# One fewer turned head (21 for 22), a new written order for the attention loop, and rows of maxima split by ScalarE and GpSimd in place of VectorE

## The chip, the core and the metric

The kernel runs on one core of one Trainium2 chip, as one program. The metric is the device time of one execution in microseconds (us), the median of several runs. TensorE (PE in the profile) multiplies matrices into PSUM, PEld is its loading of weights, VectorE is DVE, ScalarE is ACT, GpSimd is POOL, and SP is the queue that issues most DMAs.

## What is computed

One token block of 2048 rows and 448 columns: a layer norm, 16-head attention with one shared key and value (head width 28), an MLP on a second layer norm, and a sum of all.

```python
xn = _layernorm(x)
q = (xn @ wq).reshape(B, S, 16, 28).transpose(0, 2, 1, 3)
k, v = xn @ wk, xn @ wv
p = softmax(einsum("bhqd,bkd->bhqk", q, k) * 28 ** -0.5)
A = einsum("bhqk,bkd->bhqd", p, v).transpose(0, 2, 1, 3).reshape(B, S, 448) @ wo
B = gelu(_layernorm(xn) @ w1 + b1) @ w2 + b2
return x + A + B
```

All of it is float32. The kernel splits operands into a rounded high part and a low part (names ending in h and l) and adds the products.

## The kernel before

The 2048 rows are four chunks of 512 queries, the 16 heads four groups of four: a **unit** is one chunk and one group, 16 units in all, and a head of a unit is written (u, j). A score matrix is needed twice: once for the maximum of each row of queries, once with its exponentials as weights of the values.

There are three stages. First come layer norms and projections, which leave q in DRAM (`qd`) and the keys and values in SBUF (`ks`, `vs`). Then the MLP runs, 56 slots of TensorE work, and into it are mixed steps of two streams that belong to attention:

- `m`, a step of `max_stream` (lines 659 to 675): one matmul `m<-ks,qm` of 128 queries by 512 keys (L669), whose row maxima VectorE takes from PSUM (L670). A head has 16 of them. When a unit is through, its maxima are gathered in `mr` (L674).
- `t`, a step of `turned_scores` (lines 696 to 718) for a **turned** head: the same matmul (L706), but VectorE writes the scores themselves to the buffer `raw`, permuted, with their row maximum (L707, and L713 after four steps). Four `t` steps fill one `raw`. Two steps `x` (`turned_exp`, lines 720 to 730) take exponentials in place on ScalarE (L724), and after the second SP stores `raw` in DRAM as `td` by four DMAs (L727). There are two such buffers in the attention stage, so the first `t` of a chunk writes where the chunk before the last one is being stored from.

The third stage is attention, over units in order, written out by hand in the table `ORDERS`: 64 strings, four for a unit, each for four blocks of 128 keys. Each letter is one step:

- `s`, `score` (lines 1113 to 1126): for a head that isn't turned, keys by queries, one matmul `m<-xh,ks` (L1124), exponentials from PSUM into `p` on ScalarE (L1125).
- `T`, `turn_blocks` (lines 1095 to 1103): for a turned head no matmul and no exponential is left. The stored block comes back into `quarter` by DMA (L928, on SP, after a small memset L927), and VectorE transposes it in 32 by 32 squares into two `p` tiles (L1100).
- a digit: so many blocks of keys times values, `po<-p,vs` (`pv`, lines 1078 to 1093; L1088, four heads side by side in the array, eight instructions for a block).
- `m`, `t`, `x` as above; `n`, a step of the normalisation of a finished unit; `o`, four columns of the output projection (L959 to L961); `e`, `load_max` of the next unit; `|`, the next pair of blocks begins and its DMAs are issued.

So a head that is turned costs TensorE 16 matmuls (`t`) and VectorE 16 evictions and 8 transposes; one that isn't costs TensorE 32 (`m` and `s`), VectorE 16 reductions and ScalarE 16 exponentials. `TURNED` lists the turned heads, 22 of 64: head 3 of each unit, and head 2 of units 4, 7, 9, 11, 13 and 15.

`load_max` (lines 645 to 657) puts the negative maxima of a unit as two more rows under its queries, a rounded part and the rest, so that the score matmul subtracts them. TensorE turns `mr` into a row (L649), ScalarE writes the rounded part from PSUM (L652), VectorE the rest (L655), and two DMAs copy them into `qs` (L656 and L657), on POOL's queue in this stage.

PSUM has seven banks for the small results (`m0` to `m6`, by the table `BANKS`, one digit for each result) and one for `po`. Each engine runs its instructions in the order written. What a matmul waits for is thus the bank's last reader, VectorE or ScalarE.

Of the kernel before, what the change touches and what calls it, by code (L numbers as in the profile page):

```python
# [10 lines left out]
F32 = mybir.dt.float32  # L11
F32R = mybir.dt.float32r
AF = mybir.ActivationFunctionType
ALU = mybir.AluOpType
# [3 lines left out]
P = 128  # L18
S, D, H, DH, F = 2048, 448, 16, 28, 1792
NT = S // P  # L20
CT = 4
# [5 lines left out]
SCALE = DH ** -0.5  # L27
PAIRS = 13
ORDERS = (
    "ssmsmsmssTsssmmss2s|T",  # L30
    "msmsststtstTssssTsssx|",
    "|ssxTt5esmstsstmsssmsTss",
    "tsssx|Tx4tsmsssmttsstTssxs",
    "sxssTsss5mnmstsntssn|nsmsmT",
    "T|sss3smsmstmssmmsTsss",
    "snssTsms4nTeststsssnmssn|",
    "mmxn|xTsnmtmnm4nTssntmsssmstsssss",
    "Tmxss12sTsmss|ssssss",
    "2|nTmxsttsnnnstTsm2stemssssmxsss",
    "mnTssmn4nnm|xsststssttnsTmssss",  # L40
    "sxms4T|xtsmnssmsmmsstssmssT",
    "mnnTst3s|ssmsnmmsstsmsxTsss",
    "t|m3nmtsmntxsmnTsss2ssTmsssmmss",
    "tsTsm2msnmsmessnnnsstsmt|Tm2mnsmss",
    "nmsnmnsmtmmmT4mxmxsmsmssmssnsns|smTs",
    "sTs6nnTTmsm|snmsosmsnnosT",
    "sTTsTssTm|5sesss",
    "nstnsnsTsTTss4Tnt|ss",
    "smsTnT|xsmosssTmxTns4nos",
    "stssmstssmtnmsoxmx|Tssts3tststT",  # L50
    "ssTsnosTsms|m4xnestssntomsstms",
    "ssmnnmtosTmmxsssnT24xnnxnmssmmsms|ss",
    "mmmsnsssmtnttsos|nmmsnmmsstmxsTssT",
    "Txs6Tmmsmmmtmnomstsmsmsssmmnstt|nsss",
    "s|stnTxtmm3smmssxnttsxmTmsnsns3mmsss",
    "s|msTsssTmmxotmssmssmmsss",
    "Tmnnmsmnm3smstmsnemmstm3Tmmssnmss|mssts",
    "Txmmostms|msmssTnsT4Tmss",
    "mntsnsmsTTssss6nnnsT|T",
    "T|mnmensstmnsnsssTsxnTsT",  # L60
    "ssss6sTTTntmsm|Tss",
    "ss|mn1ssmtsstTsmnxxsmsssm3Tmsmtm",
    "nssts|momnxmnsTmxsTn5mestsosntntsnssms",
    "tsssmsT2smsmnsmn|smmsnmsTss",
    "ssxsmxnTsmnm3smsmms|stmsTstss",
    "TTnmmss6Tts|mnmnnmssTmsss",
    "sTsm|4TnestsmsnTssTns",
    "ssTsTssnTTxo6smnmss|",
    "snmmssxTsTsTssosTmt4nnnn|",
    "sststssssmmTsmssm|2ttmstsxmT",  # L70
    "nsxssmomn3smnmsm|smsmstsmsTsTs",
    "ts|mtTs5omstnsomosnmxmsmmmnxomtsmstssmmsxTmms",
    "m4esmnssnmstnTmtxtomnTmsmnosmmssmmssmstm|ns",
    "TtTsotstTnmssmm4nsnms|msmTs",
    "T|sstnsxTxTxms5ensnTmsnss",
    "ssnTsnxTTss5Ts|msms",
    "smssmnsmsm|TmnmsnTTTss",
    "sss2snstttssTsnt4nmtomssso|sTx",
    "nTnx|s4ensomssmsmmnsmssmsmmTssnmomosn",
    "ss|3sTtssmsnsnmsmtTtstsossm",  # L80
    "Tms4snmssmnnstsnsmstts|sTmmssx",
    "sT|ss6onTTsmnxmTonossss",
    "sTsnmsTs4msTmoTs|nmsmmts",
    "ssTsTss|Tme6sTssnt",
    "ssmsxntmsmxommnTt|mnsonmTsTsTs",
    "ssmmsxxn4snntTsmssmsm2tn|msnssmmmTs",
    "sstsnntTsxnssT7nmxsmssmmsmss|mm",
    "nsssssmsnsmmn3esTs|Tsss",
    "|ssss1nsssTsTss5ss",
    "sTTnnssTsssssnT2nn|",  # L90
    "sTsTnssssTn31sTs|",
    "Tsss|sTsosTo7Tss",
    "TT|ssssoTsssTos",
)
BANKS = (
    "0163240516324501634205163420516324510632451603245160342561034256103425160423156042315604213650241365"
    "0241365240615324061352406153204651304265130246150324610532461053246105243061524301652345014623501462"
    "3054123065412306541236054123604512306542130654201635420163542013652401365240136542061345201643502614"
    "3502641532061453620145326014352601432560124356012345061243506124356012453610243561024356102345610234"
    "6510342653106534210654312065142305631420561304526130452613045261304251634025314602351460253146023154"  # L100
    "6203145620314560231456203164520316425063142560341256304125634021653402615304261530412654310265431026"
    "5304216503426150346231504625301642503614253061254306215340621530461320546123540612345062315034162503"
    "6421036452103642510364251034621530462153064215036145206134562301456320146523106241503640215630412536"
    "0412563420514635201463520146325041632540162350421560326041532061435206415302415630241563024153620416"
    "2054136203625410356421035642103546120531426314052361402536015365420136542013562410324561034256103642"
    "5103642510326541032654130256143206512430651243506124501362450163254013562401356241053621045236415023"
    "641502364150236415023415023415023415203415203"
)
# [11 lines left out]
def block_kernel(ctx, tc, x, wq, wk, wv, wo, w1, b1, w2, b2, out):  # L120
    nc = tc.nc
    pe, act, dve, pool = nc.tensor, nc.scalar, nc.vector, nc.gpsimd
    ctx.enter_context(tc.manual_schedule())

    def f(t):
        return t.bitcast(F32)
# [10 lines left out]
    def heads_of(u):  # L137
        return 4 - sum(v == u for v, _ in TURNED)

# [438 lines left out]
    for c in range(NCH):  # L578
        if c + 1 < NCH:
            center, turn = norm_parts(c + 1, False, bank=lambda shape: (qbank, mtile)[next(turns) % 2](shape))  # L580
        for i in range(4):
# [24 lines left out]
            if i in ((1, 3), (1, 2), (1, 3), (0, 2))[c]:  # L606
# [38 lines left out]
    def load_max(u):  # L645
        qs, mr = qss[u], mrs.pop(u)
        nh = heads_of(u)
        pm = mtile([nh * CT, P])
        pe.transpose(pm, mr[:, 0:nh * CT], ident)  # L649
        mn = keep.tile([4 * CT, 2, P], F32R, name="mn", bufs=1)[0:nh * CT]  # L650
        if u:
            act.activation(mn[:, 0, :], pm, AF.Copy, scale=-1.0)  # L652
        else:
            dve.tensor_scalar(mn[:, 0, :], pm, -1.0, 0.0, op0=ALU.mult, op1=ALU.add)
        dve.scalar_tensor_tensor(mn[:, 1, :], pm, -1.0, f(mn[:, 0, :]), op0=ALU.mult, op1=ALU.subtract)  # L655
        loads.dma_start(f(qs[60:61, 0:nh, :]), f(mn[:, 0, :]))  # L656
        loads.dma_start(f(qs[124:125, 0:nh, :]), f(mn[:, 1, :]))  # L657

# [38 lines left out]
    def turned_scores(i):  # L697
        for t in range(CT):
# [5 lines left out]
            for n in range(4):  # L704
# [4 lines left out]
                                  op0=ALU.mult, op1=ALU.max, accum_out=m3[:, n:n + 1])  # L709
                if (t, n) == (0, 3) and 0 < i < len(TURNED) - 1:  # L710
                    load_m(*TURNED[i + 1], q3[1 - i % 2])
                if n == 3:
                    dve.tensor_reduce(m3[:, 4:5], m3[:, 0:4], axis=AX.X, op=ALU.max, negate=True)  # L713
                    exps.extend((TURNED[i], t, raw, m3, h) for h in range(2))
                yield
# [127 lines left out]
    for n in range(len(mslots) + 2):  # L843
# [30 lines left out]
        ts, pace = 0, 21  # L874
# [28 lines left out]
    att = ctx.enter_context(tc.tile_pool(name="att", bufs=2))  # L903
# [253 lines left out]
    for n0 in range(0, len(steps), 2):  # L1157
        u, kt0 = steps[n0]
# [67 lines left out]
```

## Time and profile before

| | |
|---|---|
| median of 3 runs | 1044.84 us (1043.79 to 1046.39) |
| the profiled execution's own time | 1043.82 us |
| its span, first to last instruction | 1041.7 us |
| granted TensorE clock | 1.00 |
| first attention score (L1124) | 482.1 us into the span |
| DMA moved | 250.65 MB |

In the rows of a profile, a group has its line, engine, operation and names (out<-in), the number of instructions, the busy time in us, the mean duration of one in ns, and the idle time of the engine ahead of it with what ended it. A matmul's end is modelled, so TensorE's busy time and the mean of 400 ns for a 512-column matmul say little; the distance from one matmul's start to the next says what it costs. A row of the timeline has start and length in us, and consecutive instructions of one kind are merged, with their count.

### The profile page before, as it was taken

Reading aid. Unit: us, or ns where it says so; the run is one execution under the profiler, and the core shown is the slowest. Engines: PE = TensorE matmul, PEld = TensorE weight load, DVE = VectorE, ACT = ScalarE, POOL = GpSimd, SP = SyncE. Lnnn points to the kernel's source line nnn. Section 1 sums busy time; section 2 is a strip of 40 time slices with the busy share of each in tenths; the row PEclk is TensorE's granted clock in tenths of the full one; section 3 lists DMA queues with packets and bytes.
Section 4 is the critical chain, followed back from the end, with each engine's and each line's share of the span. In section 5 each row is a group of like instructions: output and inputs, shape, how many; then the busy total and the mean of one; then the engine's idle time right before and its main releaser. Section 6 shows DMA issues by size and latency. Waiting matters only on the chain.

```text
span 1041.7 us, 17889 instructions
## 1 busy us (share of the span) xinstructions
PE 1032.2 (99%) x5725; PEld 701.7 (67%) x5725; DVE 944.9 (91%) x1973; ACT 727.1 (70%) x1212; POOL 576.2 (55%) x716
## 2 busy tenths in 40 slices
PE   9999999999999999999999999999999999999998
PEld 8778888888888878887454544556454465556555
DVE  7889999999999999999797999899999999997975
ACT  6765555676767756565989878777687766776782
POOL 6679787767766777866163454244444435433420
PEclk9999999999999999999999999999999999999999
DMA  8866455888988887985989899979999999998991
GB/s 275 254 209 167 126 133 147 225 219 233 244 227 216 218 219 196 258 239 164 261 243 257 242 288 301 283 209 289 283 279 313 293 287 296 293 288 284 279 344 46
DMA packets 253202, 250.65 MB, mean 241 GB/s; under 512 B 19774, under 2 KB 216508, under 8 KB 253108
## 3 DMA queue, kind: packets, MB, share of 16 engines
q1 hardware_dynamic: 240884, 229.23, 75.2%
q0 software_dynamic: 10816, 19.70, 7.1%
q8 instruction: 45, 0.74, 0.3%
q10 hardware_dynamic: 1408, 0.57, 0.2%
q14 instruction: 49, 0.40, 0.1%
HBM read 141.14 MB, written 107.07 MB: 238 GB/s over the span
## 4 chain that ended last, share of the span: by engine, by line
PE 94%; DMA 2%; DVE 2%; issue 1%; POOL 1%; ACT 1%; SPq 0%; DVEq 0%; POOLq 0%
PE po L1088 19%; PE m L1124 15%; PE m L669 15%; PE m L789 13%; PE ph L263 11%; PE m L706 8%; PE qp L263 3%; PE m L959 1%; PE ph L266 1%; PE ph L268 1%; PE m L961 1%; PE m L960 1%; DMA td<-raw 1%; PE po L1071 1%; PE m L1071 1%
## 5 line engine op out<-in xcount | busy, mean ns | idle before, releaser
L670 DVE TENSOR_REDUCE mx<-m 128x1 f32<-128x512 f32 x672 | 430.2, 682 | 31.3 <-PE m L669 29.3
L1125 ACT ACTIVATE p<-m 128x512 f32<-128x512 f32 x578 | 300.7, 633 | 55.5 <-PE m L1124 54.5
L669 PE MATMUL m<-ks,qm 128*128 128x512 f32 x672 | 257.3, 400 | 1.7 <-DVE a L794 0.7
L1088 PE MATMUL po<-p,vs 128*32 128x512 f32 x1664 | 221.2, 595 | 0.0
L1124 PE MATMUL m<-xh,ks 128*128 128x512 f32 x672 | 217.0, 407 | 0.0
L707 DVE TENSOR_SCALAR_CACHE_REDUCE raw<-m 128x512 f32<-128x512 f32 x304 | 200.7, 685 | 18.0 <-PE m L706 7.9
L1100 DVE STREAM_TRANSPOSE p<-quarter 128x1024 f32<-128x1024 f32 x149 | 178.4, 1223 | 2.2 <-DMA quarter<-td 1.7
L724 ACT ACTIVATE raw<-raw,m 128x1024 f32<-128x1024 f32 x152 | 170.8, 1164 | 3.0 <-DVE m L713 1.9
L1124 PEld LDWEIGHTS m<-xh,ks 128*128 128x128 f32 x672 | 122.3, 188 | 65.3 <-ACT p L1125 15.2
L669 PEld LDWEIGHTS m<-ks,qm 128*128 128x128 f32 x672 | 124.9, 188 | 44.8 <-issue 9.2
L706 PE MATMUL m<-ks,q 128*128 128x512 f32 x352 | 137.6, 399 | 2.0 <-DVE raw L707 1.8
L754 ACT ACTIVATE hx<-ph,b1t 128x512 f32<-128x512 f32 x55 | 37.9, 689 | 131.0 <-PE ph L268 91.5
L1088 PEld LDWEIGHTS po<-p,vs 128*32 128x32 f32 x1664 | 56.9, 109 | 106.2 <-issue 101.3
L770 POOL TENSOR_TENSOR hl<-hx,hh 128x512 fp32r<-128x512 f32 x56 | 72.7, 1298 | 31.3 <-ACT hh L768 31.1
L706 PEld LDWEIGHTS m<-ks,q 128*128 128x128 f32 x352 | 65.7, 188 | 26.5 <-DVE raw L707 4.2
L789 PE MATMUL m<-w2h,hh 128*128 128x448 f32 x224 | 81.3, 366 | 0.0
L789 PE MATMUL m<-w2h,hl 128*128 128x448 f32 x224 | 81.3, 367 | 0.0
L789 PE MATMUL m<-w2l,hh 128*128 128x448 f32 x224 | 81.2, 366 | 0.0
L758 POOL TENSOR_TENSOR hz<-hz,hx 128x512 f32<-128x512 f32 x56 | 72.8, 1300 | 4.6
L763 POOL TENSOR_TENSOR hx<-hx,hz 128x512 f32<-128x512 f32 x56 | 72.7, 1297 | 4.7
L1088 PE MATMUL po<-xh,vs 128*32 128x512 f32 x256 | 66.8, 596 | 0.0
L1125 ACT ACTIVATE xh<-m 128x512 f32<-128x512 f32 x94 | 52.0, 634 | 21.0 <-PE m L1124 20.8
(202 smaller groups left out, 1591.0 us busy)
## 6 DMA issues: line engine op xcount, KB each, us to landing
quarter<-td SPq DMA_DIRECT2D x170, 512.0 KB
td<-raw SPq DMA_DIRECT2D x304, 256.0 KB
td<-xl SPq DMA_DIRECT2D x48, 256.0 KB
qd<-qe SPq DMA_DIRECT2D x24, 256.0 KB
xh<-qd POOLq DMA_DIRECT2D x36, 168.0 KB, 6.0
a<-in_A_x_dram SPq DMA_DIRECT2D x24, 224.0 KB
qm<-qd POOLq DMA_DIRECT2D x84, 56.0 KB, 5.2
qm<-qd SPq DMA_DIRECT2D x84, 56.0 KB
```

Of the source, the lines that this page charges most:

```text
L263: pe.matmul(ps, w, v, start=(n == 0), stop=False)
L669: pe.matmul(pm, qm[:, t * P:(t + 1) * P], ks[:, n * CW:(n + 1) * CW], start=True, stop=True)
L670: dve.tensor_reduce(mx[:, CT * j + t, n:n + 1], pm, axis=AX.X, op=ALU.max)
L706: pe.matmul(sc, q3[i % 2][:, t * P:(t + 1) * P], ks[:, n * CW:(n + 1) * CW], start=True, stop=True)
L707: dve.tensor_scalar(raw[:, n].rearrange("p r (b i) -> p b r i", i=32), sc.rearrange("p (b r i) -> p b r i", r=4, i=32), SCALE, -3e38, op0= ...
L724: act.activation(raw[:, rs], raw[:, rs], AF.Exp, bias=m3[:, 4:5], scale=1.0)
L758: pool.tensor_mul(hz, hz, hx)
L789: pe.matmul(m2[k], h[:, k * P:(k + 1) * P], w[:, ft, :], start=(ft == 0 and i == 0), stop=(ft == NF - 1 and i == 2))
L1088: pe.matmul(po[32 * j:32 * j + 32, :], vs[:, kt, :], ps.pop((u, kt, j)), start=(kt == 0), stop=(kt == NT - 1))
L1100: dve.transpose(p.rearrange("p k (g j) -> p g k j", j=32), part[:, :, 32 * k:32 * k + 64].rearrange("p g (k j) -> p g k j", j=32))
L1124: pe.matmul(s, ks[:, kt * P:(kt + 1) * P], qss[u][:, j, :], start=True, stop=True)
L1125: act.activation(p, s, AF.Exp, scale=SCALE)
```

## The change

Unit 9 has one turned head instead of two, and units 10 and 11 change places: 21 turned heads. The table of steps and the table of banks are new throughout. `load_max` of units 2 to 15 has ScalarE copy the whole negative maxima to SBUF, and GpSimd makes the rounded part and the rest; units 0 and 1 use VectorE for both.

```diff
-    "ssmsmsmssTsssmmss2s|T",
+    "ssmsmsmsmmsTTss|ssss",
...
-    "0163240516324501634205163420516324510632451603245160342561034256103425160423156042315604213650241365"
+    "0163240516324503126450312645031246503215460235146023541063254120635412065342106503421650341265340126"
...
-TURNED = tuple((u, j) for u in range(16) for j in ((3, 2) if u in (4, 7, 9, 11, 13, 15) else (3,)))
+TURNED = tuple((u, j) for u in range(16) for j in ((3, 2) if u in (4, 7, 10, 13, 15) else (3,)))
...
         mn = keep.tile([4 * CT, 2, P], F32R, name="mn", bufs=1)[0:nh * CT]
-        if u:
-            act.activation(mn[:, 0, :], pm, AF.Copy, scale=-1.0)
+        if u > 1:
+            whole = att.tile([4 * CT, P], F32, name="whole", bufs=1)[0:nh * CT]
+            act.activation(whole, pm, AF.Copy, scale=-1.0)
+            pool.tensor_scalar(mn[:, 0, :], whole, 1.0, 0.0, op0=ALU.mult, op1=ALU.add)
+            pool.tensor_sub(mn[:, 1, :], whole, f(mn[:, 0, :]))
         else:
             dve.tensor_scalar(mn[:, 0, :], pm, -1.0, 0.0, op0=ALU.mult, op1=ALU.add)
-        dve.scalar_tensor_tensor(mn[:, 1, :], pm, -1.0, f(mn[:, 0, :]), op0=ALU.mult, op1=ALU.subtract)
+            dve.scalar_tensor_tensor(mn[:, 1, :], pm, -1.0, f(mn[:, 0, :]), op0=ALU.mult, op1=ALU.subtract)
```

Lines behind `load_max` stand 3 later in the changed kernel (L1124 becomes L1127). Counted through the built programs, the changed one has 688 scores `s` for 672, 688 steps `m` for 672, 336 steps `t` for 352, 168 exponentials of `raw` for 176, 168 transposes for 176, 16 stores of `td` fewer (336 for 352) and 8 loads of `quarter` fewer (162 for 170). Up to the first score TensorE's instructions are of the same kinds in the same numbers in both, 354 steps `m` and 228 steps `t` among them. From there the products `po` stand in 67 unbroken runs between other matmuls in both, and the memory of blocks waiting for them, `p`, is as large as before.

The first place is `load_max` for unit 3 in GpSimd's queue (`oc` and `oth` belong to the normalisation of the unit before, `xh<-qd` and `qm` are loads of queries, `rc`, `ld` and `tr` carry the sums of the normalisation). Before:

```order
L634 DMA xh<-qd_99 28x3x512 x2
L569 DMA qm_166<-qd_98 28x512 x2
L569 DMA qm_166<-qd_99 28x512 x2
L992 DMA rc<-oc 128x1x16
L656 DMA xh<-mn 1x12x128
L657 DMA xh<-mn 1x12x128
L996 DMA ld<-rc 128x16
L1000 DMA tr<-ld 32x512 x4
```

After, at the same unit:

```order
L634 DMA xh<-qd_98 28x3x512 x2
L995 DMA rc<-oc 128x1x16
L999 DMA ld<-rc 128x16
L654 TENSOR_SCALAR mn<-whole 12x128
L655 TENSOR_TENSOR mn<-whole,mn 12x128
L659 DMA xh<-mn 1x12x128
L660 DMA xh<-mn 1x12x128
L1003 DMA tr<-ld 32x512 x4
L569 DMA qm_164<-qd_97 28x512 x2
```

Two small operations on 12 partitions now stand ahead of the two DMAs, and the loads of the sums and of the next queries stand behind them.

The second place is the reuse of a `raw` buffer, on VectorE. The changed order has at the start of unit 6 (`raw` is written by the turned step of line 710, `mx` are maxima, the number behind m_ names the PSUM result read):

```order
L673 TENSOR_REDUCE mx<-m_7869 128x1
L673 TENSOR_REDUCE mx<-m_7875 128x1
L673 TENSOR_REDUCE mx<-m_7878 128x1
L930 MEMSET quarter 1x1
L710 TENSOR_SCALAR raw,m_7821<-m_7894 128x4x4x32
L716 TENSOR_REDUCE m_7821<-m_7821 128x1
L673 TENSOR_REDUCE mx<-m_7902 128x1
L673 TENSOR_REDUCE mx<-m_7915 128x1
L710 TENSOR_SCALAR raw,m_7919<-m_7920 128x4x4x32
```

And ScalarE there, where the row of `raw` with m_7665 is the second exponential of the buffer that the last row above writes again:

```order
L727 ACTIVATE raw<-raw,m_7665 128x1024
L968 ACTIVATE ot<-m_7852 128x448
L1128 ACTIVATE p<-m_7872 128x512
L1128 ACTIVATE p<-m_7885 128x512
L1128 ACTIVATE p<-m_7888 128x512
L1128 ACTIVATE p<-m_7891 128x512
L1128 ACTIVATE p<-m_7905 128x512
L1128 ACTIVATE p<-m_7908 128x512
```

Between the exponential and the next writing of the same buffer VectorE has eight rows, from m_7869 on; TensorE has there the matmuls of these results, and right behind the four turned matmuls a run of 40 `po` instructions. The order before has, at the place of its chunk that waited for the store (unit 5, after `load_max`), this on VectorE, from the last row ahead of the chunk on:

```order
L670 TENSOR_REDUCE mx<-m_7598 128x1
L655 SCALAR_TENSOR_TENSOR mn<-m_7620,mn 12x128
L707 TENSOR_SCALAR raw,m_7631<-m_7632 128x4x4x32
L707 TENSOR_SCALAR raw,m_7631<-m_7641 128x4x4x32
L949 MEMSET a 1x1
L670 TENSOR_REDUCE mx<-m_7647 128x1
L707 TENSOR_SCALAR raw,m_7631<-m_7656 128x4x4x32
```

The run of `po` stands ahead of the chunk there, and behind it in the new order.

More of the change, by code (lines that the diff above doesn't have):

```diff
@@ L44 @@
[L44 to L93, printed above, removed]
+    "ssmsmsmsmmsTTss|ssss",
+    "ssTTs5tsstssmtsssmsst|",
+    "sTxTmstsx4esmsmsts|mstssss",
+    "sss|tTs3sTmssmtssstmsxs",
+    "sxsT|ssm4mmsstmsnssTtsss",
+    "nsns21T|esmntsmstnsssmTsssxs",
+    "|sTn4nsmsmsststmnxssxssss3nT1",
+    "ssTmm|msnmssmmsmTnsmssx2smmsnstmn",
@@ new lines @@
+    "sstssssmtT3mmmsmsss|nTtss",
+    "ssssT|n2nsmsmstnsssmsnsT",
+    "Tmnmsxsm|4xnensmnnnssmsttssmsssTs",
+    "sssnsT4Tsmsmsmssss|sn",
+    "mtmxTms|Ttxm6mmsmsmsnnnnssssssss",
+    "|T2Tmnmsssmsmmtssnnsnsssss",
+    "|Tte2sstsnsmsttssmmtxtmmmTx4smssmsmns",
+    "|sxmsssTmTms4msmmnsmsssss",
+    "ntTsTmtssn4Tmmnnmsssm|Tmss",
+    "ssTsTsnTnons4s|tsesT",
+    "Tsssnsms|TTmnn6sTss",
+    "sTs|ssTTxmsT4mmssmnms",
+    "s|smsmmTsnnss1snsmnmtssmTss",
+    "sssmo1tmxmm|nsTm3xsntsnnmtesssstxnTss",
+    "sTmms|otx4tsomstsmoosnosssmtsTmmmsnxs",
@@ new lines @@
+    "ssT|n4mmsnssmmsmntoTstsstssxomsnmm",
+    "ssstmsssnmttstxxtn5mmssnTsss|T",
+    "|smsTnnsT4ssxmmmstttsomntesssss",
+    "mTxmmosmsnmm|smsnnsmsmmsnsm2nmnssmmTtsts",
+    "Tssmm6msmnssmttsmTsss|sss",
+    "xmTnosnmssTsssmTmm4|Tmmnmss",
+    "ssnsTTTs|msTe5mmsnmsnnmnxs",
+    "Tssms1Tn1ssTmsTs|s",
+    "Tssms2xT2stmsnssTxsnt|T",
+    "Tsss3nsmssnmnstmsssnsmsmmtT|",
+    "sss2ntsmms|mtmTsxmo3sntmsenmsomsnsTsm",
+    "stTmsxn|mx4smnssmsosmsmsmnmssTsn",
+    "TxsTsm|msn5otsnmsmssnstmstoossmms",
@@ new lines @@
+    "smtsxnmTsn4omsmmmssssmnmsTnss|s",
+    "|2sTtststsssmsmnsmsmsTxnnmss",
+    "nmsnTse5Tnsmsmsmssmss|smnsnms",
+    "mmmsTss5ntstssmmstsssn|Tss",
+    "ssxotTTonmsTssxmsmT4msmmmsn|",
+    "sTtmssmnmnomttTmtnTTnmxs|6sssms",
+    "TT|tsesmossmnmssTnmTsms",
+    "Tmnx5msTnnsms|smsmsmnTx3nxssT",
+    "sTmmmmsontstssmtsmsTstsss|s",
+    "ssTs2msmnmststsssxnTmtmxm5smsmms|",
+    "nsnsmsm|mnmsnnste2mmssnsntsstnTxTss",
+    "TTssxssm5snmsstntsn|mssmss",
+    "sxmmsmmsxss5mso|ntttssnnsTTomsnss",
+    "|Tsst4esmnssomsmssmntmsxsTss",
@@ L94 @@
+    "Tsos3smsmnsmsmssmmsnm|Tssms",
+    "TssmmTssn5smnossn|nsmnsmsmoss",
+    "Ts|tTmsmm4tnsmTsnossnssT",
+    "osmosTsnmxsnT6|TTnmsmmsss",
+    "ssTmsmToenmm|msmmnoTTssss",
+    "T|mstsm4TnxssnmmsxTmsnsnsmT",
+    "Tns51mstntsmssstsTns|ssotssmn",
+    "smnnsssxmnsnsmsTTxsm8mmssmms|ns",
+    "sssmssmnsm1nssess|TssT",
+    "ss3sss|TssTsnssss",
+    "T4TnssnsssTs|ssT",
+    "ss|2nsnnsTssss4TnTT",
+    "sT|ssTsTsssoos7To",
+    "ssTTossssTssT|",
 )
 BANKS = (
-    "0163240516324501634205163420516324510632451603245160342561034256103425160423156042315604213650241365"
@@ L107 @@
-    "641502364150236415023415023415023415203415203"
+    "0163240516324503126450312645031246503215460235146023541063254120635412065342106503421650341265340126"
+    "5341062345106234510623451062345106234165201354016235041635240156324053126453102645310246513025416302"
+    "5416305241630524163052461304562103456213054621305462310452603415260134526014325061432506142350614235"
+    "1062435160423501645023156042356041235640123564102356410235614025361402365140253160425316042351604213"
+    "6502413652041365021436052104532610543621035241356024136502431605324160532416035241603526410365241603"
@@ new lines @@
+    "5241603251463012456301246012534601253461503246150324615023461253046123504163250413625413062451632041"
+    "5632014563214053612453061243520614350264150324061532406152304612530465123046152034651204362510432605"
+    "4136205413620453160245316025431602543162054312650346152034165231064523160423516042530146302516434025"
+    "1364205341602534610542361052341650234136504231560435261435206143526041532604153260145326051342601532"
+    "4610532460153246103526413056241305623401523401652340165230451623045162305461235061435024361502463510"
@@ L108 @@
+    "2463051246035124603512460352146035214620351462035421603541206354126053142065314206531240562314056321"
+    "4506342165403216540321654032165403215403215403215403210543215"
 )
-TURNED = tuple((u, j) for u in range(16) for j in ((3, 2) if u in (4, 7, 9, 11, 13, 15) else (3,)))
+TURNED = tuple((u, j) for u in range(16) for j in ((3, 2) if u in (4, 7, 10, 13, 15) else (3,)))
 RAWS = 2
```

23 lines of the change are left out of this document (removed).

## Prediction

> **What bounds the kernel now.** I read the page's busy times first, then the busy times by stretch, then TensorE's timeline, then the groups and the waits of the attention stretch.
>
> ```profile
> PE 1032.2 (99%) x5725; PEld 701.7 (67%) x5725; DVE 944.9 (91%) x1973; ACT 727.1 (70%) x1212; POOL 576.2 (55%) x716
> ...
> PE 94%; DMA 2%; DVE 2%; issue 1%; POOL 1%; ACT 1%; SPq 0%; DVEq 0%; POOLq 0%
> ```
>
> TensorE is busy 99% of the span and is 94% of the chain that ended last, but a matmul's end is modelled and VectorE is near 91%, so this alone doesn't say which of the two sets the time. In the stretches, the columns are length, then busy time and count of PE, PEld, DVE, ACT and POOL, the granted clock, the DMA share and GB/s:
>
> ```profile
> 105.00:470.00 365.00, 364.39 (x1650) 306.21 (x1649) 347.13 (x811) 233.76 (x316) 272.49 (x265) 1.00 0.79 207
> ...
> 482.00:1002.00 520.00, 517.46 (x3147) 277.13 (x3146) 472.71 (x899) 404.09 (x745) 214.49 (x333) 1.00 0.92 278
> ```
>
> In the MLP stretch, 105 to 470 us, there are 1650 matmuls in 365 us, 0.221 us from start to start on the mean. How close that is to TensorE's own pace shows the timeline of TensorE alone, here in attention:
>
> ```profile
> 747.58 5.36 PE L1088 MATMUL po<-p,vs 128*32 128x512 f32 x48
> 752.87 0.50 PE L1124 MATMUL m<-xh,ks 128*128 128x512 f32 x1
> 753.20 0.39 PE L706 MATMUL m<-ks,q 128*128 128x512 f32 x1
> 753.43 0.40 PE L669 MATMUL m<-ks,qm 128*128 128x512 f32 x1
> ...
> 754.13 1.07 PE L1124 MATMUL m<-xh,ks 128*128 128x512 f32 x4
> 755.04 0.39 PE L669 MATMUL m<-ks,qm 128*128 128x512 f32 x1
> 755.36 0.62 PE L1088 MATMUL po<-xh,vs 128*32 128x512 f32 x2
> ```
>
> Four matmuls from 754.13 to 755.04 are 0.23 us each, and 753.20 to 753.43 is 0.23 too: that is the pace of a 512-column matmul with nothing in its way. The first behind a `po` run takes 0.33 (752.87 to 753.20) and the last ahead of one 0.32 (755.04 to 755.36), so a switch costs about 0.19 us. A run of 48 `po` takes 5.29 us, 0.110 each. So the MLP stretch, at 0.221 a matmul with shorter ones among them, is TensorE back to back. For attention I add up the counts of 482 to 1002 us:
>
> ```profile
> L1088 PE MATMUL po<-p,vs 128*32 128x512 f32 x1648 | 219.2, 595 | 0.0
> L1124 PE MATMUL m<-xh,ks 128*128 128x512 f32 x640 | 208.2, 407 | 0.0
> L669 PE MATMUL m<-ks,qm 128*128 128x512 f32 x318 | 117.5, 406 | 0.7 <-DVE a L794 0.7
> L1088 PE MATMUL po<-xh,vs 128*32 128x512 f32 x256 | 66.8, 596 | 0.0
> L706 PE MATMUL m<-ks,q 128*128 128x512 f32 x124 | 47.7, 406 | 1.8 <-DVE raw L707 1.8
> L959 PE MATMUL m<-xl,oth 128*128 128x448 f32 x48 | 17.7, 369 | 0.0
> ...
> L649 PE MATMUL m<-ident,mr 128*12 128x128 f32 (+1 forms) x15 | 4.1, 273 | 0.0
> ```
>
> 1082 matmuls by 0.23 are 248.9 us; 1904 `po` by 0.110 are 209.4; some 66 switches by 0.19 are 12.5; 144 of the output projection (L959 to L961, 48 each) by the 0.221 of the MLP stretch are 31.8; the 15 of L649 are 4.1. Together 506.7 of 520 us. What is left, some 13 us, holds all of TensorE's waits there, and what many short `po` runs cost more than one of 48. TensorE is the bound in attention as well, with about 2.5% to be had; VectorE, 472.7 of 520, comes second.
>
> **The change, part by part.** Everything before 482 us keeps its instructions, so the terms come from attention alone.
>
> *The head that is no longer turned, on TensorE.* Its 16 steps `t` become 16 steps `m`, at the same 0.23. To these come 16 scores `s`: 16 x 0.23 = **+3.7 us**, on the engine that bounds. The runs of `po` are 67 in both, so switches cost the same. Nothing hides this term, since TensorE has no idle time to put it into but its own waits.
>
> *The same head on VectorE, ScalarE and the DMA queues.*
>
> ```profile
> L670 DVE TENSOR_REDUCE mx<-m 128x1 f32<-128x512 f32 x318 | 203.1, 679 | 28.3 <-PE m L669 27.9
> L1100 DVE STREAM_TRANSPOSE p<-quarter 128x1024 f32<-128x1024 f32 x138 | 165.5, 1224 | 2.2 <-DMA quarter<-td 1.7 <-PE po L1088 0.2
> L707 DVE TENSOR_SCALAR_CACHE_REDUCE raw<-m 128x512 f32<-128x512 f32 x124 | 82.1, 679 | 9.4 <-PE m L706 4.0 <-PE m L1124 2.6 <-DMA td<-raw 2.0
> ...
> L707 DVE DVE_READ_ACCUMULATOR raw<-m 128x1 f32 x124 | 10.2, 82 | 0.0
> L713 DVE TENSOR_REDUCE m<-m 128x1 f32<-128x4 f32 x31 | 4.9, 157 | 1.1
> ...
> L655 DVE SCALAR_TENSOR_TENSOR mn<-m,mn 12x128 fp32r<-12x128 f32 (+1 forms) x15 | 4.1, 274 | 5.9 <-ACT mn L652 4.7 <-DMA tr<-ld 1.1
> ```
>
> VectorE loses 16 x (679 + 82) ns and 4 x 157, 12.8 us; it gains 16 x 679, 10.9; it loses 8 transposes of 1224, 9.8. ScalarE:
>
> ```profile
> L1125 ACT ACTIVATE p<-m 128x512 f32<-128x512 f32 x548 | 285.1, 632 | 52.1 <-PE m L1124 51.2
> L724 ACT ACTIVATE raw<-raw,m 128x1024 f32<-128x1024 f32 x62 | 72.3, 1190 | 3.0 <-DVE m L713 1.9 <-issue 1.1
> ...
> L652 ACT ACTIVATE mn<-m 12x128 fp32r<-12x128 f32 (+1 forms) x15 | 3.9, 262 | 10.3 <-PE m L649 10.2
> ```
>
> It gains 16 x 632 and loses 8 x 1190, +0.6 us, and is busy 404 of 520: free. SP loses 16 stores and 8 loads of a head's 4 MB each way, some 8 MB at 278 GB/s, 30 us of the transfers of a stretch whose DMA share is 0.92. That shortens no chain of its own, but it lets stores land sooner.
>
> *The rows of maxima.* VectorE loses 14 operations of 274 ns, 3.8 us, and the waits for ScalarE in front of them (4.7 us of its idle time); unit 1 gives it one more of about that size, 0.3. ScalarE's copy replaces one of the same shape, 262 ns. So VectorE's work falls by 12.8 - 10.9 + 9.8 + 3.8 - 0.3 = **15.2 us** of 473. GpSimd gets 14 pairs on 12 partitions by 128. No row has that size on it; the nearest are
>
> ```profile
> L376 POOL TENSOR_SCALAR xn<-a,lnrq,lnqb 128x64 f32<-128x64 f32 x4 | 1.6, 398 | 1.9 <-ACT xn L372 0.9 <-DMA raw<-in_B_w_dram 0.9
> ...
> L248 POOL TENSOR_TENSOR wah<-pair,wah 64x64 fp32r<-64x64 f32 x1 | 0.4, 377 | 0.1
> ...
> POOL xh L656 <- ACT mn L652: 67.5, 14, 11.3
> ```
>
> that is 0.4 us each, 0.8 for a pair as an estimate, below 1.6 at twice that, and against it stand the 0.27 us of VectorE's operation, for which the second DMA no longer waits. So the rows of maxima land about 0.5 us later (between 0 and 1.3). Behind them on GpSimd's queue stand loads of sums and of the next queries. GpSimd already stands still there for ScalarE, 67.5 us in 14 times, 4.8 us each, and TensorE's own list of waits names neither it nor these DMAs:
>
> ```profile
> PE m L706 <- DVE raw L707: 1.8, 2, 1.5
> PE m L669 <- DVE a L794: 0.7, 1, 0.7
> ```
>
> I take 0. Without the cover it would be 14 x 0.5 = 7 us at most, at the first score of a unit; the new order keeps `e` some 10 us of TensorE's work or more ahead of that score, so I don't believe it.
>
> *What the new order gives back.* The 15 us less on VectorE can shorten only waits of TensorE, and those are the 13 us above: the gain lies between 0 and 13. The evictions of VectorE are one of several causes; ScalarE's exponentials free banks as well, and some of the 13 is not waiting. I take a third, **-4 us**.
>
> The sum is +3.7 - 4 = -0.3, made against the profiled execution: 1043.8 - 0.3 = 1043.5. The median of the runs lies 1.0 above that execution, so the forecast median is **1044.5 us**: no change that can be told, since about 0.3%, 3.1 us, is what a measurement of this kernel can tell.
>
> Here a rule of the Trainium skill speaks otherwise. Perfetto Trace Analysis, section Identifying the Most-Contended Engine, says that TensorE's headroom is judged by the share of weight loading and not by matmul busy time, and the other engines by their occupancy. In 482 to 1002 us that is 277.1 of 520, 53%, against 91% for VectorE; by it VectorE is the bound, and the time would fall by its whole 15.2 us to 1029.6. The starts 0.23 us apart speak against it: by them only 13 us can go at all.
>
> **The rivals.** *First: VectorE is in the way more than I think.* Then nearly all of TensorE's waits go, say 10 of the 13: 1043.8 + 3.7 - 10 + 1.0 = 1038.5 us. For it: VectorE is at 91%, and TensorE's only named waits end on VectorE. Against it: these named waits are 2.5 us in all. With every wait gone it is 1035.5. To the rule above, as a mechanism (VectorE alone sets the pace, 1029.6), I give 0.02, within this rival's chance.
>
> *Second, slower: the store of `raw` is waited for at two places.* The profile before has one such wait. In the chain, and in VectorE's waits:
>
> ```profile
> 647.99 0.32 SPq L727
> ...
> 650.46 7.94 DMA td<-raw
> 658.53 0.71 DVE raw L707 x2
> 659.29 0.50 PE m L706
> ...
> DVE raw L707 <- DMA td<-raw: 2.0, 1, 2.0
> ```
>
> From the first store's issue, right after the exponential, to the next writing of the buffer are 10.5 us, the last 2.0 of them VectorE waiting, and TensorE lost 1.5 us by it. The new order has at the start of unit 6 only five `m`, one `t` and small rows between the exponential and that writing, 6 x 0.68 + 0.24 = 4.3 us of VectorE's work, and at the start of unit 5's third string 3 `t`, 3 `m` and 2 transposes, some 7 us. Against 10.5 these leave 6.2 and 3.5 us of standing still. At the loss of before, 1.5 for 2.0, TensorE would lose 7.3 us: 1043.8 + 3.7 - 4 + 7.3 + 1.0 = 1051.8. It decides when VectorE's standing still outlasts the `po` run behind the chunk: 40 `po` by 0.110 are 4.4 us at the first place, 32 by 0.110 are 3.5 at the second. With these as cover only 6.2 - 4.4 and 0 are left, 1.8 us. For the rival: before, the distance on VectorE was longer. Against it: the cover, and fewer stores in flight.
>
> *Third: the new order waits as much as the old.* The work of VectorE falls, but its letters are packed so that waits stay: 1043.8 + 3.7 + 1.0 = 1048.5 us, slower by 0.35%.
>
> **How the numbers follow.** The forecast has 0.52; VectorE in the way 0.22; the stores 0.14; no relief 0.12. The forecast's own range is 1042 to 1047.5. A faster time needs waits down by 6.8 of 13 us; this comes from the first rival, 0.22. Slower comes from the second, most of the third, and a little of the forecast's upper end: 0.24. Within 0.3% stays 0.54. The range takes in most of the first and the third rival and the nearer half of the second: 1038.5 to 1050.
>
> **What would show it.** The `s` matmuls (688) still 0.23 us apart and 520 us of attention changed by less than 3 us would show the sum right. VectorE's busy time should fall by 15 us, some of it turning into idle time that `PE m` ends. If TensorE's remainder by the same count (506.7 + 3.7) is far below 9 us, the first rival is right. A wait of VectorE on `td<-raw` of over 4 us at the start of unit 6, with a gap of TensorE behind it, shows the second. A remainder of 13 or more without such a wait shows the third. A score waiting for the rows of maxima at a unit's start would show the zero for `load_max` wrong.

## The result, and the profile after

The changed kernel takes 1049.96 us in the median (1048.50 to 1050.70) beside 1044.78 (1043.79 to 1046.39) of the kernel before: ratio 1.0058, interval 1.0042 to 1.0074, slower by 4.4 to 7.7 us, with 6.1 in the middle. The two medians lie 5.2 us apart. The profiled executions have 1048.5 and 1043.8 us, spans of 1046.7 and 1041.7. The forecast of 1044.5 said no change.

The page of the changed kernel, busy times and the shares of the chain:

```profile
PE 1035.1 (99%) x5741; PEld 702.2 (67%) x5741; DVE 932.9 (89%) x1928; ACT 726.0 (69%) x1219; POOL 586.7 (56%) x744
...
PE 95%; DMA 1%; DVE 1%; ACT 1%; issue 0%; SPq 0%; POOL 0%; ACTq 0%; DVEq 0%
```

Its two stretches, with the columns as before:

```profile
105.00:470.00 365.00, 364.41 (x1649) 306.29 (x1649) 347.71 (x810) 233.57 (x316) 272.50 (x265) 1.00 0.79 208
...
482.00:1002.00 520.00, 516.25 (x3126) 276.90 (x3126) 457.15 (x851) 400.14 (x746) 224.18 (x361) 1.00 0.88 259
```

The MLP is as it was, so the 5 us are in attention. There VectorE worked 457.2 us for 472.7, 15.6 less; TensorE started 3126 matmuls in the same 520 us, where it had started 3147, although more were to be done.

I then split attention as the prediction did, with the paces taken finer from the long runs of the trace: 0.231 us for a 512-column matmul, 0.107 for a `po`, 0.203 for one of the output projection, 0.34 more for each run of `po`, 0.27 for L649. Counts by paces are the **base**; the rest up to the measured length is the **remainder**, waits above all. From the first score to the first score of unit 15:

| | length | base | remainder | in units 0, 1, 5, 6, 10, 12, 14 |
|---|---|---|---|---|
| before | 520.0 | 508.4 | 11.6 | 1.9, 0.4, 2.4, 1.4, 1.1, 0.5, 0.5 |
| after | 524.8 | 512.1 | 12.7 | 1.7, 2.0, 0.8, 0.9, 0.4, 1.3, 2.4 |

The base is up by 3.7, as 16 scores by 0.231 should make it. The remainder was to fall by 4 and rose by 1.1: it went down by 3.0 in units 0, 5, 6 and 10 and up by 4.3 in units 1, 12 and 14, and the other units give 0.2 back. The two largest places have a name in TensorE's and VectorE's waits of the stretch:

```profile
DVE mx L673 <- PE m L672: 40.4, 41, 3.1
...
DVE raw L710 <- PE m L709: 8.9, 7, 2.9
...
DVE raw L710 <- DMA td<-raw: 4.2, 2, 2.6
...
DVE a L952 <- DMA out_dram<-a: 2.3, 1, 2.3
...
PE m L1127 <- DVE mx L673: 1.8, 1, 1.8
...
PE m L672 <- DVE raw L710: 1.3, 1, 1.3
```

The first is where VectorE's free time went: its reductions waited 40.4 us for TensorE's matmul, 27.9 before. These 12.5 us are most of the 15.6: they became idle time that TensorE ends. The last two are TensorE's own. The longer, in unit 14, in the timeline:

```profile
980.98 0.07 DVE L952 MEMSET a<- 1x1 f32 x3
...
981.12 0.34 SPq L973 DMA_DIRECT2D out_dram<-a  x1
...
981.39 0.62 PE L1127 MATMUL m<-xh,ks 128*128 128x512 f32 x2
981.56 2.23 SPq L953 DMA_DIRECT2D a<-ad  x4
...
981.89 0.50 PE L672 MATMUL m<-ks,qm 128*128 128x512 f32 x1
...
983.38 0.06 DVE L952 MEMSET a<- 1x1 f32 x1 [2.33 <-DMA out_dram<-a]
...
983.42 1.29 DVE L673 TENSOR_REDUCE mx<-m 128x1 f32<-128x512 f32 x2
...
984.17 0.73 PE L1127 MATMUL m<-xh,ks 128*128 128x512 f32 x2 [1.77 <-DVE mx L673]
```

`load_rows_of` (L952) fetches the four rows of the last chunk into the four buffers `a`, each marked by a memset on VectorE. The fourth buffer was being stored since 981.12, and the memset stood in VectorE's queue until 983.38. Behind it stood the reductions that free TensorE's banks: TensorE lost 1.77 us. In the kernel before no row waits: its last store was issued 12 us ahead of the last memset. The memsets and stores there (number, durations, first and last start):

```profile
L949 DVE MEMSET a<- x16: 59/59/59, 622.0 to 979.4; 1x1 f32 x16
...
L970 SPq DMA_DIRECT2D out_dram<-a x12: 338/374/2229, 678.3 to 967.5; - x12
```

The lines of the rule are the same in both kernels ("at the 14th pair of blocks from the end"); the new order put the last output projection right in front of it.

The other wait is one for the store of `raw`, in unit 1, where I had not looked for it:

```profile
515.93 3.37 SPq L730 DMA_DIRECT2D td<-raw  x4
...
526.33 0.69 DVE L710 TENSOR_SCALAR_CACHE_REDUCE raw<-m 128x512 f32<-128x512 f32 x1 [1.62 <-DMA td<-raw]
526.67 0.29 POOL L654 TENSOR_SCALAR mn<-whole 12x128 fp32r<-12x128 f32 x1
...
527.04 0.45 POOL L655 TENSOR_TENSOR mn<-whole,mn 12x128 fp32r<-12x128 f32 x1
527.08 0.19 PEld L672 LDWEIGHTS m<-ks,qm 128*128 128x128 f32 x1 [1.70 <-DVE raw L710]
527.08 0.50 PE L672 MATMUL m<-ks,qm 128*128 128x512 f32 x1 [1.28 <-DVE raw L710]
```

From the store's first issue to the buffer's next writing are 10.4 us, as in the row of before; no run of `po` covers it, and TensorE lost 1.28. At the start of unit 6, the second rival's first place, the same wait stands and costs nothing:

```profile
679.14 3.05 SPq L730 DMA_DIRECT2D td<-raw  x4
...
683.69 2.78 PE L1091 MATMUL po<-p,vs 128*32 128x512 f32 x24
...
686.13 0.69 DVE L710 TENSOR_SCALAR_CACHE_REDUCE raw<-m 128x512 f32<-128x512 f32 x1 [2.55 <-DMA td<-raw]
...
688.12 0.73 PE L672 MATMUL m<-ks,qm 128*128 128x512 f32 x2
```

VectorE stands still for 2.55 us, and TensorE goes through its 40 `po` from 683.69 to 688.12 meanwhile.

### The profile page after: what moved, and what is told of

Read it like the earlier page. It is cut to its first block, busy times and chain, and to the rows that moved or that the text cites. A ratio compares the mean times of both kernels' runs of the same rounds, so it can differ in the third digit from the quotient of the medians.

```text
span 1046.7 us, 17845 instructions
## 1 busy us (share of the span) xinstructions
PE 1035.1 (99%) x5741; PEld 702.2 (67%) x5741; DVE 932.9 (89%) x1928; ACT 726.0 (69%) x1219; POOL 586.7 (56%) x744
## 4 chain that ended last, share of the span: by engine, by line
PE 95%; DMA 1%; DVE 1%; ACT 1%; issue 0%; SPq 0%; POOL 0%; ACTq 0%; DVEq 0%
PE po L1091 20%; PE m L1127 16%; PE m L672 15%; PE m L792 12%; PE ph L263 11%; PE m L709 8%; PE qp L263 3%; PE m L962 1%; PE ph L266 1%; PE ph L268 1%; PE m L964 1%; PE m L963 1%; DMA td<-raw 1%; PE po L1074 1%; PE m L1074 1%; PE qp L387 1%
## 5 line engine op out<-in xcount | busy, mean ns | idle before, releaser
L673 DVE TENSOR_REDUCE mx<-m 128x1 f32<-128x512 f32 x688 | 440.3, 682 | 43.7 <-PE m L672 41.8
L1128 ACT ACTIVATE p<-m 128x512 f32<-128x512 f32 x594 | 309.0, 630 | 83.0 <-PE m L1127 81.7
L672 PE MATMUL m<-ks,qm 128*128 128x512 f32 x688 | 263.2, 401 | 3.3 <-DVE raw L710 1.3
L1127 PE MATMUL m<-xh,ks 128*128 128x512 f32 x688 | 218.7, 406 | 1.8 <-DVE mx L673 1.8
L710 DVE TENSOR_SCALAR_CACHE_REDUCE raw<-m 128x512 f32<-128x512 f32 x288 | 190.5, 686 | 22.7 <-PE m L709 11.9
L1103 DVE STREAM_TRANSPOSE p<-quarter 128x1024 f32<-128x1024 f32 x142 | 171.1, 1228 | 2.2 <-DMA quarter<-td 1.7
L1127 PEld LDWEIGHTS m<-xh,ks 128*128 128x128 f32 x688 | 125.2, 188 | 68.4 <-ACT p L1128 15.0
L727 ACT ACTIVATE raw<-raw,m 128x1024 f32<-128x1024 f32 x144 | 162.0, 1162 | 1.6 <-DVE m L716 0.8
L709 PE MATMUL m<-ks,q 128*128 128x512 f32 x336 | 131.5, 399 | 0.2 <-DVE mx L673 0.2
L1091 PE MATMUL po<-xh,vs 128*32 128x512 f32 x256 | 69.7, 597 | 0.0
L759 POOL TENSOR_SCALAR hz<-hz 128x512 f32<-128x512 f32 x56 | 35.0, 625 | 56.0 <-ACT hz L758 55.8
```

Of the source, the lines that this page charges most:

```text
L672: pe.matmul(pm, qm[:, t * P:(t + 1) * P], ks[:, n * CW:(n + 1) * CW], start=True, stop=True)
L673: dve.tensor_reduce(mx[:, CT * j + t, n:n + 1], pm, axis=AX.X, op=ALU.max)
L709: pe.matmul(sc, q3[i % 2][:, t * P:(t + 1) * P], ks[:, n * CW:(n + 1) * CW], start=True, stop=True)
L710: dve.tensor_scalar(raw[:, n].rearrange("p r (b i) -> p b r i", i=32), sc.rearrange("p (b r i) -> p b r i", r=4, i=32), SCALE, -3e38, op0= ...
L727: act.activation(raw[:, rs], raw[:, rs], AF.Exp, bias=m3[:, 4:5], scale=1.0)
L1091: pe.matmul(po[32 * j:32 * j + 32, :], vs[:, kt, :], ps.pop((u, kt, j)), start=(kt == 0), stop=(kt == NT - 1))
```

## The experiments

Ratios are to the kernel before on the same chip, with 95% intervals; 0.001 is 1.04 us. A stretch is the length of the table above. The theory at the start: the 16 scores cost their 3.7 us, and the waits did not fall because TensorE and not VectorE sets the pace. The rivals: the scores are free and single new waits make it slower; or the relief of VectorE was real and the new order spent it.

### The row loads two steps later: 1.0030

```diff
-        if n == len(steps) - 14:
+        if n == len(steps) - 12:
```

> The changed kernel, in which the rows of the last chunk are loaded two pairs of key blocks later (step 116 of 128 instead of 114). In its profile VectorE's small memset in front of that load waits 2.3 us for the store of an earlier chunk's rows out of the same buffer, at 981 to 983 us, and TensorE loses 1.8 us by it. Theory 1 with single waits on top: that wait goes and the time falls by 1.5 to 2 us, to 1048.2. Rival (the order as a whole waits, and another wait takes its place): within 0.7 us of the changed kernel.

1046.46 us, ratio 1.0030 (1.0018 to 1.0042): 2.9 us faster than the changed kernel (plus or minus 2.1, the two intervals taken as independent). Unit 14 takes 37.0 us for 39.2, its remainder is 0.3 for 2.4. In the timeline no memset is left between the matmuls, and TensorE runs on to its `po`:

```profile
980.86 0.34 SPq L973 DMA_DIRECT2D out_dram<-a  x1
...
981.32 0.69 DVE L673 TENSOR_REDUCE mx<-m 128x1 f32<-128x512 f32 x1
...
981.95 0.65 PE L1127 MATMUL m<-xh,ks 128*128 128x512 f32 x2
...
982.44 0.39 PE L672 MATMUL m<-ks,qm 128*128 128x512 f32 x1
...
982.76 2.78 PE L1091 MATMUL po<-p,vs 128*32 128x512 f32 x24
```

So a part of the loss is one wait for a store, shown by moving it. The ratios put it at 2.9 us, about half, with a wide interval; the stretch puts it at 2.0 (522.8 for 524.8).

### The 16 scores, added to the kernel before: 1.0019 and 1.0020

One kernel doubles the 16 scores of one head of unit 9, the other one score of each unit:

```diff
         s = mtile([P, CW])
+        if (u, j) == (9, 1):          # the other: if (kt, j) == (8, 1):
+            pe.matmul(s, ks[:, kt * P:(kt + 1) * P], qss[u][:, j, :], start=True, stop=True)
```

> The kernel before, with the 16 score matmuls of head 1 of unit 9 issued twice into the same bank; nothing else is added, and VectorE, ScalarE and the DMAs have the same work. Theory 1 (TensorE's own work sets the time): 16 x 0.23 us = 3.7 us slower than before, 1048.5. Rival (VectorE or ScalarE set the pace around unit 9 and TensorE has room): 0 to 1 us slower.

> The kernel before with one score matmul of each of the 16 units issued twice (key block 8, head 1): 16 matmuls more, spread over the stage; all other work and the result are the same. Theory 1: 3.0 to 3.7 us slower than before, more than the 2.0 of e1_twice16, whose 16 stood in one unit and used up a wait of that unit. Rival (half of them go into waits): 1 to 2 us slower.

1045.72 us, ratio 1.0019 (1.0009 to 1.0029), and 1046.28, 1.0020 (1.0008 to 1.0031): +2.0 and +2.1 us. With the scores spread, the stretch is 522.1 for 520.0, its base up by 3.5 and its remainder down from 11.6 to 10.3. With all of them in unit 9, its remainder went from 0.7 to -0.4 and the unit from 30.1 to 32.7. (The trace of this kernel is its longest execution, 1048.6 us; most of what it has over the median is in unit 5, 40.0 us for 37.6, with its wait for a store.) A matmul that is put in takes its 0.23 us. Of that, about a third comes out of waits that were there by the stretch, and nearly half by the ratios. The whole 3.7 us is outside both intervals; the +2.1 is nearest to the rival of the second expectation.

### The 16 scores taken out of the changed kernel: 1.0058, 1.0041, 1.0047 in one unit, 1.0004 spread

The first leaves out the 16 matmuls of head (9, 2) and lets its exponentials read another head's bank; the second leaves out its 16 exponentials alone; the third both. The three edits in outline, drawn together:

```diff
+        if (u, j) == (9, 2):
+            places.pop(0)
+            s = seen[0]                       # matmuls out
...
+            ps[u, kt, j] = ps[u, kt, 1]       # exponentials out
```

> The changed kernel with 16 matmuls fewer: the exponentials of head 2 of unit 9 read the scores of head 1 from the same bank (so that head's weights are head 1's); every exponential, eviction and DMA stays. Theory 1: 3.7 us faster than the changed kernel, about 1046.2, that is 1.5 us above before, what the waits of the new order cost. Rival (the new order waits for VectorE, ScalarE or the stores, and the matmuls hide in that): within 1 us of the changed kernel, 1049 to 1050.

> The changed kernel with those 16 matmuls kept and the 16 exponentials left out (weights of head 2 of unit 9 are head 1's): ScalarE has 10.1 us less in a unit of 34.7 us. Theory 1: within 1 us of the changed kernel. Rival B (ScalarE paces unit 9): 2 to 4 us faster than it.

> The changed kernel without the score matmuls and without the exponentials of head 2 of unit 9 (its weights are head 1's): 16 matmuls and 16 exponentials of 0.63 us fewer. The run with the matmuls alone left out saved nothing, and there two exponentials shared a bank. Theory 1 (TensorE's matmuls are what the head costs): 3.0 to 3.7 us faster than the changed kernel. Rival A (something of the order paces unit 9, neither TensorE nor ScalarE): within 1 us of it. Rival B (ScalarE paces unit 9, which has 48 exponentials in 34.7 us): also 3 us or more faster; the next run tells the two apart.

Without the matmuls: 1050.26 us, 1.0058 (1.0046 to 1.0070), nothing saved. Unit 9 keeps its length (34.8 for 34.7) with a base 3.7 lower: the remainder is 4.7 for 0.9. By its expectation that is the rival. But here a bank is held for two exponentials, and in unit 9 TensorE waits for them, of which the changed kernel's list has none:

```profile
PE m L1132 <- ACT p L1134: 1.0, 2, 0.7
PE m L672 <- ACT p L1134: 0.9, 3, 0.3
PE m L1132 <- ACT xh L1134: 0.3, 1, 0.3
```

So this kernel doesn't tell what I wanted. Without the exponentials: 1048.35, 1.0041 (1.0029 to 1.0053), 1.8 us less. Without both: 1048.15, 1.0047 (1.0029 to 1.0065), 1.1 less. Neither gain is beyond its interval, and the 3.0 to 3.7 us of theory 1 for the last kernel did not come. In it unit 9 is 1.3 shorter, with a remainder of 3.2 for 0.9, and unit 10 is 1.1 longer. The waits of TensorE and VectorE around unit 10, 822 to 866 us, where the changed kernel has neither of the two:

```profile
DVE raw L710 <- DMA td<-raw: 1.0, 1, 1.0
...
PE m L649 <- DVE mx L673: 0.3, 1, 0.3
```

Of the 3.7 us taken out, 2.4 came back in the remainder of unit 9 and 1.1 in that of unit 10. The two waits name a part of the second; the rest is in no wait that I followed. So I took the work out everywhere, one score of each unit with its exponential, from the kernel with the later rows:

```diff
+        if (kt, j) == (8, 1):
+            places.pop(0)
+            ps[u, kt, j] = ps[u, kt, 0]
+            return
```

> The changed kernel with the rows of the last chunk loaded two steps later, and one score in each unit (head 1, block 8) left out with its exponential, 16 scores and 16 exponentials spread over the whole attention stage; the products of these blocks use head 0's weights instead, so this work of the computation is left out. Theory (16 matmuls more are paid on TensorE where they fall, and half goes into waits that are there anyway, as in the run with 16 scores doubled): 1.5 to 2.2 us faster than the kernel with the rows later, about 1044.4 us, the stretch from the first score to unit 15 down by about 2 with the matmuls' share down by 3.7. If the whole term is on the path: 3.0 to 3.7 us faster, about 1043. Rival (the 16 extra scores cost next to nothing where they are spread, and the new order is slower for its waits alone): at most 0.8 us faster, about 1046.

An expectation for the same change of the kernel stands on record from before the doubled scores were measured in every unit: 3.0 to 3.7 us faster. That first form gave no time; the expectation above was written with the +2.1 us known.

1044.30 us, ratio 1.0004 (0.9994 to 1.0013), 2.7 us less than with the later rows (plus or minus 1.6). The stretch is 520.9 for 522.8, the base 3.5 lower, the remainder 1.6 higher. The 2.7 us lie between the theory's half and its whole, the stretch's 1.9 in its half; the rival, 0.8 at most, is out by the ratios. The exponentials went with the scores, and no run takes the two apart here: the 16 exponentials of unit 9 alone gave 1.8 us, within the interval of nothing. With the later rows and without these scores the changed kernel has the time of the kernel before.

### VectorE relieved in the kernel before: 0.9985

The new `load_max`, and the 8 transposes of head (9, 2) left out, 13.6 us of VectorE's work in all.

```diff
+        if (u, j) != (9, 2):
-        dve.transpose(p.rearrange("p k (g j) -> p g k j", j=32),
+            dve.transpose(p.rearrange("p k (g j) -> p g k j", j=32),
```

> The kernel before and its order, with VectorE's work cut by about the amount of the change and no matmul more: the rows of maxima made by ScalarE and GpSimd (14 operations of 274 ns, 3.8 us), and the 8 transposes of head 2 of unit 9 left out (9.8 us; the weights of this head are then what stood in the buffers). The step of the prediction (a third of such relief comes back out of TensorE's waits): 3 to 4 us faster than before, 1041. Theory 1 (TensorE seldom waits for VectorE's amount of work): within 1 us of before.

1043.07 us, 0.9985 (0.9976 to 0.9994), 1.6 us less. The stretch is 519.1 for 520.0, with 0.6 of it in unit 9. VectorE's row for it:

```profile
482.00:1002.00 520.00, 517.75 (x3151) 277.41 (x3150) 462.16 (x878) 404.61 (x746) 224.88 (x362) 1.00 0.92 278
```

VectorE is busy 10.5 us less than the 472.7 of before (13.6 by the prices of the single operations, some of which overlap in the trace). About an eighth of the 13.6 reaches the time, 0.6 to 2.5 us by the interval.

### The old rows of maxima in the changed order: 1.0035

The kernel with the later rows, and `load_max` as before.

> The changed kernel with the rows loaded later (e4_rows_later), and with the rows of maxima made as before the change, the rest by VectorE. VectorE has 3.8 us more. Theory 1 (TensorE is waited for, VectorE has room): within 1 us of e4_rows_later. Rival (the relief of VectorE is worth a third of its size or more): 1.3 us or more slower than it.

1046.94 us, 1.0035 (1.0023 to 1.0048), 0.5 us more than with the new one, which the intervals don't tell from nothing.

### The wait for `raw` taken away in each kernel: 1.0024 and 0.9979

In the changed kernel, with the later rows, one `t` and one `m` of unit 1 exchanged; in the kernel before, two pairs of unit 5, with the new `load_max`:

```diff
-    "nsns21T|esmntsmstnsssmTsssxs",
+    "nsns21T|esmnmsmstnssstTsssxs",
...
-    "ssTsnosTsms|m4xnestssntomsstms",
+    "ssTsnosTsms|m4xnesmssnmotsstts",
```

> The changed kernel with both single waits of its profile treated: the rows of the last chunk loaded at step 116 as in the run before, and in unit 1 a turned step exchanged with a maximum step 7 letters later, so that the raw buffer is written some 1 to 2 us later (VectorE waited 1.6 us for its store there, TensorE 1.3). Theory 1: the run with the rows alone gave 2.9 us; this gives 1 to 1.3 more, 1045.2 to 1046, which leaves 1 to 2 us above before: less than the 3.7 of the matmuls, since before has single waits of its own. Rival (waits only move): the same as with the rows alone, 1047.

> The kernel before with its one wait for a store treated in the same way (unit 5: two turned steps exchanged with two maximum steps, the first write of the buffer some 2 us of TensorE's work later; VectorE waited 2.0 us there, TensorE 1.5), and with the rows of maxima made by ScalarE and GpSimd. Theory 1: 1.5 to 2.4 us from the wait, up to 0.7 from the rows of maxima: 1041.2 to 1042.2, ratio 0.997 to 0.998. Rival (waits only move): within 1 us of before.

Changed kernel: 1046.23 us, 1.0024 (1.0013 to 1.0035), no difference to 1.0030 that can be told. VectorE's wait for the store in unit 1 is gone, but unit 1's remainder is 1.5 for 1.8, and units 5 and 8 got 0.5 each. So the 1.28 us that the trace put on this wait did not come off the time when it was moved, as the rival said. Kernel before: 1041.97 us, 0.9979 (0.9971 to 0.9988), faster than both kernels by 2.2 us and more. Unit 5 takes 36.5 for 37.6, and VectorE's list has no wait for a store of `raw` any more; TensorE's are

```profile
PE m L672 <- DVE a L797: 0.7, 1, 0.7
PE m L709 <- DVE raw L710: 0.6, 1, 0.6
PE m L672 <- DVE raw L710: 0.3, 1, 0.3
```

Two edits lie in it, and no run takes them apart.

### One more turned head in each: 1.0170 and 1.0195

If a score costs its 0.23 us, one head more should give 3.7 us back. The improved kernel before got a 23rd turned head, and the changed kernel (later rows) its 22nd, both (14, 2), with the letters of the order exchanged by hand: `m` to `t` in the units where its 16 blocks are made, `x` behind them, `s` to `T` in unit 14. Two of some twenty strings of the first:

```diff
-    "sTs6nnTTmsm|snmsosmsnnosT",
+    "sTs6nnTTtst|sntsostsnnosT",
-    "sstsnntTsxnssT7nmxsmssmmsmss|mm",
+    "sstzTnntTsxnszT7nmxsmszTmmsmsz|mm",
```

(`z` marks a score that is left out for a `T`.)

> The mirror of the change, on the run e8_before_fixed: head 2 of unit 14 is turned as well (23 heads). Its 16 scores leave unit 14, 8 transposes come in, and 16 of the steps m, spread over units 4, 7, 9 and 11, become t with their exponentials and stores. TensorE has 16 x 0.23 = 3.7 us less, VectorE some 12 us more. Theory 1 (TensorE's matmuls set the time as long as no single wait is added): 3 to 3.7 us faster than e8_before_fixed, about 1038.5. Rival (VectorE is so close behind TensorE that a turned head gives nothing, as the runs with a lighter unit 9 suggest): within 1 us of e8_before_fixed, or slower.

> The changed kernel with the rows of the last chunk loaded later (as in e4_rows_later) and head 2 of unit 14 turned: 22 turned heads again, in the new order, 16 steps m become t in units 3, 6, 10 and 12. Theory 1: 3 to 3.7 us faster than e4_rows_later, about 1043, so that with the row wait gone and the head back the change is undone in time. Rival (VectorE close behind, or the order): within 1 us of e4_rows_later.

1060.46 us, 1.0170 (1.0149 to 1.0192), and 1064.04, 1.0195 (1.0181 to 1.0209): both far slower. The base fell as it should, 508.4 to 504.7 and 512.1 to 508.4; the remainder rose from 11.0 to 33.2 and from 10.7 to 32.0. In the first of them TensorE waits, over the longer stretch from 482 us on:

```profile
PE m L1127 <- ACT p L1128: 6.7, 6, 1.6
PE po L1091 <- DVE quarter L930: 2.5, 1, 2.5
PE m L709 <- DVE mx L673: 1.3, 1, 1.3
PE m L672 <- DVE mx L673: 1.0, 1, 1.0
```

The first line wasn't in the list of either kernel. An exponential of `raw` takes 1.19 us on ScalarE for 0.63 of a score's; that the scores' banks come late behind it is my reading and is not shown by a run. Only a part of the 22 us is named; by units the remainder is largest in 11, 12 and 14 (6.1, 4.4 and 6.9 us). What these runs show is that letters exchanged by hand lose more than a head is worth; what a good order would make of that head stays open.

## Why the prediction was wrong, point by point

- **What bounds the kernel: right.** TensorE is nearly back to back, the MLP unchanged, the remainder before 11.6 by the finer paces (13 in the prediction, which priced a matmul of the output projection at 0.221 us for 0.203). The Trainium skill's rule (Perfetto Trace Analysis, section Identifying the Most-Contended Engine) judges TensorE's headroom by MFU, the matmul work done as a share of the peak, as well as by weight loading. The prediction took weight loading alone; that the whole 15 us would then come off the time is its own step and not the page's. The runs disagree with that reading: 13.6 us less of VectorE's work alone gave 1.6.
- **+3.7 for 16 scores: the mechanism right, the size over.** The base rose by 3.7. In the time 16 scores are worth 2.0 and 2.1 put into the kernel before, and 2.7, with their exponentials, taken out of the changed one all over the stage. "Nothing hides this term, since TensorE has no idle time to put it into but its own waits": by these runs the waits hid a quarter to nearly half, and most of it where one unit was relieved.
- **VectorE's 15.2 less: right** (15.6), and it turned into idle time ended by `PE m`, as said.
- **-4 for "what the new order gives back": this step failed.** It took a third of the 13 us as waits that a lighter VectorE shortens, whatever the order. The relief alone gave 1.6 on the old order, at 13.6 us. In the new order TensorE's remainder did not fall by 4 but rose by 1.1, and it is 10.7 when the wait of unit 14 is gone, 0.9 under before. The wait of unit 14, which was followed up, hangs on where a single step stands and not on VectorE's load, and the new order made it.
- **The wait that nobody priced.** I looked for new waits at the reuse of `raw` only. The row buffers `a` are reused in the same way, four buffers and a store, and their memset is on VectorE; it cost 2.9 us (plus or minus 2.1) by the ratios, 2.0 by the stretch. The prediction's sum has no term for a new wait, and it did not look at these buffers. The third rival ("the new order waits as much as the old", 1048.5) is the nearest, but it had no such mechanism, and its time is below the one measured.
- **The second rival: its cover was judged right.** VectorE waited 2.55 us at the start of unit 6, and the 40 `po` hid it; the 10.5 us from issue to reuse were 7.0 there. The place in unit 5 showed no wait for the store. The same wait without a cover stood in unit 1, where the prediction had not looked; taking it away changed nothing that can be told.
- **0 for the rows of maxima: right.** The pair takes 0.29 and 0.45 us, 0.74 for my 0.8 (9 of the 14 pairs are on 12 partitions, 5 on 8, at the same price), no score waited, and the old one in its place gave 0.5 us more, not told from zero.

By the ratios the loss of 6.1 us (1.0058) is 2.9 for the row loads and 2.7 for the 16 scores with their exponentials, which leaves 0.4, within the last ratio's interval. By the stretch, one execution each, the 4.8 us are 2.0, 1.9 and 0.9. With intervals of 1.6 to 2.1 us the two sizes are rough. Why the lighter VectorE bought so little in the new order is open: the remainders by unit say only where, and the one run of the new order with 22 heads added waits of its own.

## What to carry to other kernels

When a change brings a new order, list every buffer whose next writer waits for a store, not only the one that waited before, and see for each whether a stretch of work that needs nothing from that engine stands behind it: 40 `po` hid 2.55 us, none hid 1.62. Count waits as a supply that belongs to places and not to an engine's load: relieving an engine that is 91% busy gave an eighth of its work back, and moving one load by two steps gave 2 to 3 us. But a wait that a trace names is not yet time to be had: of two such waits in the changed kernel that were moved, one gave its size and the other nothing that can be told. Work added to the bounding engine, or taken from it all over the stage, counted here for half to three quarters of its price, and for less than a third where it was taken from one unit; the rest came out of waits or turned into them.

## What the runs showed of the hardware

- The store of one `raw` by four DMAs, from its first issue to the buffer's next writing, took 10.4 us in unit 1 and 7.0 in unit 6 of the same execution; in four kernels with the old order VectorE's wait for it in unit 5 was 2.0 to 3.1 us, and the unit 37.6 to 40.0 us long. A wait for a store isn't a fixed price.
- An operation of GpSimd on 12 partitions by 128 takes 0.29 us with one operand and 0.45 with two, in 9 of each; on 8 partitions by 128 it takes the same, in 5 of each.
